# One fused Trainium2 kernel, its five queues in another order, its last token rows evicted in two parts and two early evictions moved to VectorE

## The chip, the cores and the metric

The kernel runs on one core of one Trainium2 chip. The core has five engines with a queue each, worked off strictly in order: TensorE (PE in the profile, its weight loads PEld), VectorE (DVE), ScalarE (ACT), GpSimd (POOL) and SyncE (SP), which here only issues DMA transfers. The metric is the device time of one execution in microseconds, as the median of several runs.

## What is computed

One transformer-like block on 2048 tokens of width 640, in bfloat16: a layer norm of `x`, a long convolution gated by it, a residual; then a layer norm and a gated feed-forward network of width 1728 with a residual.

```python
k_shift = sum over t of k_pad[:, t:t + S, :] * shift_k[:, ks - 1 - t]      # ks = 4 taps
kv = k_shift * v
y = irfft(rfft(kv, 2 S) * rfft(ssm_k, 2 S))[:S] + kv * ssm_D               # along the tokens
h = x + layernorm(x) * y
out = h + (silu(n @ w_gate) * (n @ w_up)) @ w_down      with n = layernorm(h)
```

## The kernel before

The 2048 tokens are four blocks of 512. Each block goes through the same stages:

- `kv(i)` (L673): k comes in transposed (`kT`), four taps are applied as matmuls with diagonal matrices in three groups (two 128-column pairs, then one alone); ScalarE evicts each group to `kT` (L700 in block 0, L717 later). In block 0 TensorE transposes them back and VectorE multiplies by v into `vt` (L713). In blocks 1 to 3 five DMA transposes (`kvt`, L486) bring them into `kvo`, and VectorE multiplies by v into `vt` (L726).
- `xfwd(i)` (L728): Fourier matmuls of `vt` with the table `ftab` into `XH[i]` (matmuls L584, evictions L597, butterflies L554; block 2 uses the shorter form, L622, L628, L632).
- `prod(j, i)` (L745): VectorE multiplies block j's spectrum with filter spectrum `C[i-j]` and adds into `Y` (L755, L756, L761, L771). The last product is followed by butterflies into `IO` and `IE`.
- `inverse(i)` (L819): inverse Fourier matmuls from `IE` and `IO` (L832), gating with the normalized x, the second layer norm's statistics on ScalarE (L870, L872), VectorE and GpSimd (L883), and four DMA transposes (`hn`, L486) into `hnT`.
- `ffn(i)` (L898): 13 groups of gate and up matmuls (L913, L914) and one half-size group (L924); per group ScalarE evicts silu(gate) (L936) and up (L938, into one of two buffers `ub` in turn), VectorE multiplies (L940). Then the down projection by token rows j = 0, 2, 1, 3 (L956), with one small paired matmul group for rows 0 and 2 and one for rows 1 and 3 (L968). Blocks 0 to 2 evict it by ScalarE (L976) and add on VectorE (L983); block 3 does both in one VectorE instruction (L986). One DMA per row writes the output (L990).

Ahead of that, `kload`, `ktrans` and `kfwd` (called kt0 to kt3 and kf0 to kf3 here) make the filter spectra `C[m]`, and `ln1(i)` makes the first layer norm.

PSUM is four tiles of two banks. A TensorE task that opens a tile waits until the tile's former users have read it.

Every `g.add(...)` makes a task, numbered as it is made. `ORDER` lists for each engine the numbers in the order in which its queue holds them. `schedule` walks through these lists with costs and latencies written down in the code; it assigns PSUM tiles, and it puts small filler matmuls (L249) into TensorE's waits that it foresees in the first stages. It doesn't change the order. `emit` turns data dependencies into semaphore waits. So a task waits for its data, and everything behind it in the same queue waits too.

The task numbers that matter below:

| tasks | what they are |
|---|---|
| 20, 24, 28 / 21, 25, 29 | block 0's three conv groups on TensorE / their evictions |
| 22, 26, 30 / 23, 27, 31 | their transposes on TensorE / products with v on VectorE |
| 137 to 148 | statistics of block 0's four token rows: two halves and an aggregation each, on VectorE |
| 110 to 113, 130 to 133 | last butterflies of kf2 and kf3 on VectorE |
| 128 / 129 | last Fourier group of kf3 / its eviction |
| 182, 188 / 183, 189 | butterflies into the two halves of `IO` / of `IE`, block 0 |
| 190 to 193 | inverse matmuls of block 0 (191 and 193 read `IO`) |
| 363 to 370 | product of blocks 0 and 1 |
| 338, 271, 279 | a small step of ln1 and two gate products of ff0 on VectorE |
| 297, 301, 306 | down projection of block 0, rows 2, 1 and 3 |
| 302 | paired group for rows 1 and 3 of block 0, opens a tile |
| 515, 516, 517 | block 2's third conv eviction, the DMA transpose of what it wrote, the product into `vt` that needs this transpose |
| 573 | a product of blocks 1 and 2 on VectorE (L755) |
| 536 to 550, even | Fourier matmuls of block 2 |
| 436, 442, 448, 454 | gate products (436, 448) and silu evictions (442, 454) of ff1 |
| 501, 710, 779 | last residual of block 1, load of block 3's x, a product on VectorE (L771) |
| 636, 637, 638, 730 | ff2's second gate-and-up group, its silu and its up eviction; a statistics pass of ln3 |
| 679, 683, 690 / 836 | the last gate products and the last small one of ff2 / a gating product of inverse 3 |
| 691, 692, 693 | down projection of block 2, row 0 in two pieces; pair of rows 0 and 2 |
| 804 to 807 | inverse matmuls of block 3, rows 0 to 3 |
| 814, 824, 828, 839 | ScalarE steps of block 3's second layer norm |
| 825, 816, 843, 834 | the four DMA transposes hn3, rows 1, 0, 3 and 2 |
| 892, 896 | block 3's 13th gate-and-up group and the half-size one |
| 906, 909, 913 / 907, 910, 914 | block 3's evictions of rows 0, 2, 1 / their output DMAs |
| 915, 916, 917 | row 3: matmuls, eviction, output DMA |

Of the kernel before, what the change touches and what calls it, by code (L numbers as in the profile page):

```python
# [10 lines left out]
ALU = mybir.AluOpType  # L11
ACTF = mybir.ActivationFunctionType
P = 128
# [10 lines left out]
class _Task:  # L24
    __slots__ = ("eng", "fn", "cost", "lat", "deps", "after", "succ", "npred", "ready", "end", "start",
                 "opens", "tiles", "idx", "clock", "sem", "seq", "dma", "name", "gap", "lock", "fill", "late", "pause")
# [32 lines left out]
class _Graph:  # L59
# [38 lines left out]
    def add(self, eng, name, fn, cost, r=(), w=(), pr=(), pw=(), skip=(), lat=None, dma=None, after=(), lock=None):  # L98
        t = _Task()
# [10 lines left out]
        t.late = set()  # L110
        t.seq = len(self.tasks)
# [118 lines left out]
    def emit(self, block):  # L230
# [85 lines left out]
    """,  # L316
    "act": """
# [12 lines left out]
    """,  # L330
    "dve": """
# [10 lines left out]
    """,  # L342
    "pool": """
        5 6 10 11 8 7 9 151 202 195 209 205 216 198 212 219 134 336 135 421 403 394 412 529 610 628 601 619 736 822 813 840
        831
    """,
    "sp": """
# [722 lines left out]
```

## Time and profile before

| | us |
|---|---|
| median of 3 runs | 270.15 |
| lowest and highest | 269.49, 270.49 |
| the profiled execution's own time | 269.68 |
| its span, first to last instruction | 267.8 |
| TensorE busy | 254.6 |
| ScalarE busy | 206.8 |
| VectorE busy | 201.7 |
| GpSimd busy | 28.7 |

The granted clock of TensorE was 0.998 over the span. The stages overlap: the filter spectra and block 0's transform fill the first 52 us, ff0 begins at 52.11, ff1 at 112.54, ff2 at 169.15 and ff3 at 219.91; the last matmul group starts at 260.87. In the profile a row of the timeline gives start and duration in microseconds, engine, line, operation, output and inputs by name, the shape, and in brackets the idle time before it with what ended that. In a row of grouped instructions the numbers behind the bar are busy time, mean nanoseconds of one, and idle time before them. In a row of waits the numbers are the sum, the count and the longest.

### The profile page before, as it was taken

To read this page: it belongs to the slowest core of one execution; us is meant where nothing else is said; L and a number is where in the kernel's file an instruction comes from. 1 tells how busy PE (TensorE), PEld (TensorE's weight loads), DVE (VectorE), ACT (ScalarE), POOL (GpSimd) and SP (SyncE) were. 2 spreads that over 40 slices of the span, in tenths; PEclk is the share of its full clock that TensorE was granted. 3 is DMA by queue.
4 is the path that set the end of the run, shared out by engine and by line. 5 is a ranking of instruction groups with operands and counts; after the bars stand their busy time and mean duration, and the time that the engine had idled before them with its cause. 6 is when DMAs were issued, how large, how long until landed. Compare 5 with 4: busy or idle time off the path is not lost.

```text
span 267.8 us, 4162 instructions
## 1 busy us (share of the span) xinstructions
PE 254.6 (95%) x1635; PEld 140.1 (52%) x1635; DVE 201.7 (75%) x282; ACT 206.8 (77%) x394; POOL 28.7 (11%) x37
## 2 busy tenths in 40 slices
PE   7899898999999998899899999999999989999995
PEld 5466563445445655444346567544446654444563
DVE  1599999999999998899999999999994000042204
ACT  2799999989887979948989997689799965346400
POOL 1000306011140042000040202000200200000000
PEclk9999999999999999999999999999999999999999
DMA  6999809959755637452000445500000150010004
GB/s 171 345 351 379 316 16 257 143 119 321 137 94 102 103 77 147 98 183 88 2 0 3 100 83 137 174 0 1 0 2 0 19 82 0 0 51 0 0 2 148
DMA packets 43557, 28.47 MB, mean 106 GB/s; under 512 B 32273, under 2 KB 41234, under 8 KB 43538
## 3 DMA queue, kind: packets, MB, share of 16 engines
q1 hardware_dynamic: 41824, 25.58, 35.4%
q0 software_dynamic: 1056, 2.62, 5.4%
q8 instruction: 13, 0.21, 0.3%
q10 hardware_dynamic: 658, 0.01, 0.1%
q14 instruction: 6, 0.05, 0.1%
HBM read 15.69 MB, written 2.62 MB: 68 GB/s over the span
## 4 chain that ended last, share of the span: by engine, by line
PE 41%; ACT 32%; DVE 15%; DMA 5%; SPq 2%; issue 2%; POOL 1%; ACTq 0%; DVEq 0%
PE ps L913 13%; PE ps L914 13%; PE ps L956 8%; PE ps L584 5%; ACT xh L815 4%; ACT ub L938 3%; ACT qo L856 3%; DMA vt<-in_A_v_dram 3%; DVE T L755 3%; ACT qo L872 3%; ACT qo L870 2%; DVE T L761 2%; ACT KT L545 2%; ACT gu L936 2%; DVE gu L940 2%; ACT qo L888 2%
## 5 line engine op out<-in xcount | busy, mean ns | idle before, releaser
L956 PE MATMUL ps<-Wd,gu 128*128 128x384 bf16 (+1 forms) x416 | 59.1, 300 | 0.1
L913 PE MATMUL ps<-hnT,GA 128*128 128x512 bf16 x140 | 53.1, 379 | 1.2 <-DMA hnT<-qo 0.7
L914 PE MATMUL ps<-hnT,UA 128*128 128x512 bf16 x140 | 53.1, 379 | 0.0
L956 PEld LDWEIGHTS ps<-Wd,gu 128*128 128x128 bf16 x416 | 39.9, 98 | 18.1 <-issue 1.6
L913 PE MATMUL ps<-hnT,GB 128*128 128x512 bf16 x120 | 45.5, 379 | 0.7 <-ACT gu L936 0.7
L914 PE MATMUL ps<-hnT,UB 128*128 128x512 bf16 x120 | 45.5, 379 | 0.0
L936 ACT ACTIVATE gu<-ps 128x512 bf16<-128x512 f32 x52 | 30.6, 598 | 17.8 <-PE ps L914 17.6
L938 ACT ACTIVATE ub<-ps 128x512 bf16<-128x512 f32 (+1 forms) x60 | 33.1, 566 | 6.6 <-PE ps L914 3.4
L940 DVE TENSOR_TENSOR gu<-gu,ub 128x512 bf16<-128x512 bf16 x52 | 21.0, 419 | 22.2 <-ACT ub L938 19.6
L755 DVE TENSOR_TENSOR T<-X,C 128x2560 bf16<-128x2560 bf16 x20 | 29.7, 1486 | 0.3
L756 DVE TENSOR_TENSOR T<-X,C 128x2560 bf16<-128x2560 bf16 x20 | 29.7, 1485 | 0.1
L913 PEld LDWEIGHTS ps<-hnT,GA 128*128 128x128 bf16 x140 | 13.7, 98 | 18.1 <-DMA hnT<-qo 1.0
L883 POOL TENSOR_TENSOR mv<-mv,half 128x1 f32<-128x1 f32 x16 | 15.3, 965 | 70.7 <-ACT mv L876 70.7
L584 PE MATMUL ps<-KT,ftab 128*128 128x320 bf16 x128 | 20.5, 301 | 2.0 <-DMA ftab<-cst_ftab 0.9
L914 PEld LDWEIGHTS ps<-hnT,UA 128*128 128x128 bf16 x140 | 13.7, 98 | 15.5
L913 PEld LDWEIGHTS ps<-hnT,GB 128*128 128x128 bf16 x120 | 11.7, 98 | 15.5 <-ACT gu L936 1.7
L761 DVE TENSOR_TENSOR T<-T 128x1280 bf16<-128x1280 bf16 x24 | 19.3, 819 | 0.2
L914 PEld LDWEIGHTS ps<-hnT,UB 128*128 128x128 bf16 x120 | 11.7, 98 | 13.8
L806 POOL TENSOR_TENSOR st<-st,half 128x8 f32<-128x8 f32 x4 | 9.1, 2267 | 91.2 <-ACT st L800 91.2
L771 DVE TENSOR_TENSOR Y<-Y,T 128x2560 bf16<-128x2560 bf16 x12 | 17.8, 1485 | 0.1
L584 PEld LDWEIGHTS ps<-KT,ftab 128*128 128x128 bf16 x128 | 10.3, 97 | 10.7 <-DMA ftab<-cst_ftab 1.4
L815 ACT ACTIVATE xh<-xh,st 128x640 bf16<-128x640 bf16 x16 | 14.5, 933 | 1.6 <-DVE st L808 1.6
(94 smaller groups left out, 372.8 us busy)
## 6 DMA issues: line engine op xcount, KB each, us to landing
kc<-in_A_ssm_k_dram SPq DMA_DIRECT2D x4, 640.0 KB, 9.2
xh<-in_A_q_dram SPq DMA_DIRECT2D x4, 640.0 KB, 4.2
vt<-in_A_v_dram SPq DMA_DIRECT2D x4, 640.0 KB, 6.3
out_dram<-xh SPq DMA_DIRECT2D x16, 160.0 KB, 1.9
Wd<-in_B_w_down_dram SPq DMA_DIRECT2D x1, 1280.0 KB, 6.5
C<-C POOLq DMA_DIRECT2D x1, 1280.0 KB, 13.6
C<-R POOLq DMA_DIRECT2D x1, 1280.0 KB, 9.4
UA<-in_B_w_up_dram SPq DMA_DIRECT2D x1, 1120.0 KB, 9.1
```

What stands on the lines that cost most here:

```text
L584: last = e.matmul(pt.f(c, W), ftab[:, cs, j, f * P:(f + 1) * P], src[:, j, c * W:(c + 1) * W], start=(j == par), stop=(j == par + 2))
L755: g.add("dve", nm, lambda e, x=x, k=k, t1=t1: e.tensor_tensor(out=t1, in0=x, in1=k, op=ALU.mult), cdve(2560), r=[x, k], w=[t1])
L756: g.add("dve", nm, lambda e, x=x, k=ksw, t2=t2: e.tensor_tensor(out=t2, in0=x, in1=k, op=ALU.mult), cdve(2560), r=[x, k], w=[t2])
L761: g.add("dve", nm, lambda e, p=p, q=q, d=d, op=op: e.tensor_tensor(out=d, in0=p, in1=q, op=op), cdve(1280), r=[p, q], w=[d])
L771: g.add("dve", nm, lambda e, y=y, z=z: e.tensor_tensor(out=y, in0=y, in1=z, op=ALU.add), cdve(2560), r=[y, z], w=[y])
L815: g.add("act", nm, lambda e, j=j, xj=xj: e.activation(out=xj, in_=xj, func=ACTF.Identity, scale=s[:, 4, j:j + 1], bias=s[:, 5, j:j + 1]), ...
L913: e.matmul(pt.f(0, N), wg[:, c, f0:f0 + P], hnT[:, c, :], start=(c == 0), stop=(c == NC5 - 1))
L914: last = e.matmul(pt.f(1, N), wu[:, c, f0:f0 + P], hnT[:, c, :], start=(c == 0), stop=(c == NC5 - 1))
L936: g.add("act", nm, lambda e, pt=pt, gv=gv, a=ps_g, ts=ts: e.activation(out=gv, in_=pt.f(a[0], N, a[1])[:, ts], func=ACTF.Silu, scale=gain) ...
L938: g.add("act", nm, lambda e, pt=pt, uv=uv, a=ps_u, ts=ts: e.activation(out=uv, in_=pt.f(a[0], N, a[1])[:, ts], func=ACTF.Copy, scale=gain) ...
L940: g.add("dve", nm, lambda e, uv=uv, gv=gv: e.tensor_tensor(out=gv, in0=gv, in1=uv, op=ALU.mult), cdve(n), r=[gv, uv], w=[gv])
L956: last = e.matmul(pt.flat(c1 - c0, P + c0), slots[fb][:, j * P:(j + 1) * P], Wd[:, fb, c0:c1], start=(fb == 0 and not second), stop=(fb == ...
```

## The change

All five queues get another order. Two evictions (tasks 21 and 129) go from ScalarE to VectorE, by a list `VECTOR` and a helper `evict` that stands in for the `g.add("act", ...)` calls of the filter, conv and transform evictions. The down projection of the very last token rows (block 3, j = 3) is split into columns 0 to 383 and 384 to 639, each with its own 13 matmuls, VectorE eviction and output DMA: tasks 915 to 917 and 918 to 920. The costs that the planner writes down for loads and transposed loads are other numbers, which set nothing on the chip but the choice of PSUM tiles, the filler matmuls and a few extra waits on VectorE. Three more places (a buffer `ZB`, the sign of `neg` and the subtraction at L847) depend on lists (`ACC`, `ST`) that hold no entry for them, so they add no instruction.

```diff
 ORDER = {
     "pe": """
-        13 35 32 24 20 28 49 43 41 22 39 47 26 51 37 65 30 45 164 162 160 158 63 60 170 168 166 108 172 84 78 58 76 68 72 82
...
+        13 32 35 20 24 28 22 41 43 37 47 51 26 39 49 45 30 65 160 162 164 158 172 168 170 166 58 63 60 80 68 84 76 86 78 70 82
...
-        345 343 349 244 357 353 355 256 351 268 252 260 264 276 284 272 280 386 388 291 387 385 292 506 510 293 514 301 302
-        297 306 550 542 540 546 536 548 429 544 538 425 437 445 433 441 453 461 469 449 457 477 465 473 593 595 484 592 594
...
+        347 349 244 256 355 351 357 264 353 252 260 268 276 272 280 284 386 388 387 385 291 506 292 510 293 514 297 301 302
+        536 306 540 550 538 542 548 425 546 544 429 445 437 433 453 449 441 461 457 469 477 465 473 593 595 594 484 592 485
...
-        680 684 805 807 804 691 692 806 693 701 697 702 706 844 848 864 868 852 860 856 872 876 880 884 888 896 892 903 904
-        905 911 908 912 915
+        684 805 807 804 691 806 692 693 701 702 706 697 868 856 848 864 844 852 860 876 884 872 888 880 892 896 903 904 905
+        911 912 908 915 918
     "act": """
...
-        814 824 815 829 841 830 842 832 833 698 707 694 845 846 849 850 703 865 853 854 862 861 857 858 866 877 873 874 870
...
+        739 681 678 673 740 674 685 686 817 689 688 835 682 819 808 820 810 821 837 811 823 812 838 826 824 814 828 839 815
...
     "dve": """
-        12 15 16 137 138 139 34 140 141 142 143 144 145 23 146 147 27 31 53 148 54 55 56 149 174 175 178 179 180 176 181 177
-        184 185 182 187 186 152 153 188 183 90 189 88 201 194 208 215 93 206 91 199 89 213 92 220 363 364 112 366 110 132 365
-        111 130 133 113 131 325 326 324 235 368 367 239 243 369 359 251 370 360 371 372 247 373 374 361 362 375 337 255 379
...
+        12 16 15 34 21 137 138 139 140 141 142 143 23 144 27 145 146 31 147 53 55 54 56 148 174 149 175 178 179 176 181 180
+        177 152 185 184 187 186 153 188 182 189 183 201 90 215 194 208 88 129 206 89 220 91 199 92 213 93 130 363 364 365 366
+        367 112 110 132 326 325 324 235 111 113 239 243 133 131 368 369 359 251 370 360 247 372 371 259 373 361 374 362 375
...
-        871 883 891 879 899 887 902 895 909 913 906 916
+        863 871 879 875 887 883 891 899 895 902 906 909 916 913 919
     "sp": """
...
-        504 508 505 512 509 513 424 516 397 296 406 415 309 300 305 503 712 711 716 715 720 613 719 723 489 498 631 604 622
-        502 493 710 825 816 843 834 700 696 910 709 705 907 914 917
+        231 505 509 508 513 512 516 406 397 424 415 305 300 309 296 503 711 712 720 715 716 719 723 613 622 604 631 489 498
+        493 502 710 825 816 843 834 907 709 700 705 696 917 910 914 920
...
+VECTOR = """
+    21 129
+"""
...
+        def evict(name, out, src, n, w, pr, scale=1.0, bias=None, r=(), after=()):
+            if len(g.tasks) in on_vector:
+                if bias is None and scale == 1.0:
+                    fn = lambda e: e.tensor_copy(out=out, in_=src())
+                elif bias is None:
+                    fn = lambda e: e.tensor_scalar(out=out, in0=src(), scalar1=scale, scalar2=None, op0=ALU.mult)
...
+                t = g.add("dve", name, fn, cps(n), r=r, w=w, pr=pr)
+            else:
+                kw = {"func": ACTF.Copy} if bias is None else {"func": ACTF.Identity, "bias": bias}
+                t = g.add("act", name, lambda e: e.activation(out=out, in_=src(), scale=scale, **kw), cact(n, bias is not None),
+                          r=r, w=w, pr=pr, after=after)
...
+                for c0, c1 in ((0, 3 * P), (3 * P, D)) if tail else ():
...
+                        for fb in range(last_fb):
+                            last = e.matmul(pt.flat(c1 - c0, P + c0), slots[fb][:, j * P:(j + 1) * P], Wd[:, fb, c0:c1],
+                                            start=False, stop=(fb == last_fb - 1))
...
+                    g.add("dve", nm, lambda e, pt=pt, xs=xs, m=m, c0=c0, c1=c1: e.scalar_tensor_tensor(
+                        out=xs, in0=pt.flat(c1 - c0, P + c0), scalar=m, in1=xs, op0=ALU.subtract, op1=ALU.add),
+                          cps(c1 - c0) + 60, r=[xs, m], w=[xs], pr=[pt])
+                    g.add("sp", "out%d" % i, lambda e, xs=xs, od=od[:, c0:c1]: e.dma_start(od, xs), 350, r=[xs], dma=((c1 - c0) * 0.74, 0), lat=1000)
```

More of the change, by code (lines that the diff above doesn't have):

```diff
@@ L25 @@
     __slots__ = ("eng", "fn", "cost", "lat", "deps", "after", "succ", "npred", "ready", "end", "start",
-                 "opens", "tiles", "idx", "clock", "sem", "seq", "dma", "name", "gap", "lock", "fill", "late", "pause")
+                 "opens", "tiles", "idx", "clock", "sem", "seq", "dma", "name", "gap", "lock", "fill", "late", "pause", "alt")
 class _Tile:
@@ L110, in add @@
         t.late = set()
+        t.alt = None
         t.seq = len(self.tasks)
@@ L544, in ktrans @@
                 dst = KT[m][:, jj:jj + 3:2, :]
-                g.add("act", "kt%d" % m, lambda e, pt=pt, dst=dst: e.activation(out=dst, in_=pt.h2(D), func=ACTF.Copy), cact(1280),
-                      w=[dst], pr=[pt], after=first_act)
+                evict("kt%d" % m, dst, pt_view(pt, lambda p: p.h2(D)), 1280, [dst], [pt], after=first_act)
                 if m == 0 and jj == 0:
@@ L675, in kv @@
             if i == 0:
-                tload("kT0", kT[:, :, 16:N + 16], K2[0:N, :], N, D, 2400)
+                tload("kT0", kT[:, :, 16:N + 16], K2[0:N, :], N, D, 1700, wait=700)
             else:
@@ L699, in kv @@
                 if i in PT:
-                    g.add("act", nm, lambda e, pt=pt, ks=ks, nb=nb: e.activation(out=ks, in_=pt.f2(N)[:, 0:nb], func=ACTF.Copy),
-                          cact(N * nb), w=[ks], pr=[pt])
+                    evict(nm, ks, pt_view(pt, lambda p, nb=nb: p.f2(N)[:, 0:nb]), N * nb, [ks], [pt])
                     tp = g.tile("kt")
@@ L753, in prod @@
                 t1, t2 = pair(u[0], u[1]), pair(u[2], u[3])
-                out = [T[:, u[0]], T[:, u[2]]] if j else [y[:, i % 2], y[:, 1 - i % 2]]
+                far = (j, i) in ACC and i == 3
+                out = [T[:, u[0]], T[:, u[2]]] if j and not far else [(ZB[:, f2] if far else y)[:, c] for c in (i % 2, 1 - i % 2)]
                 g.add("dve", nm, lambda e, x=x, k=k, t1=t1: e.tensor_tensor(out=t1, in0=x, in1=k, op=ALU.mult), cdve(2560), r=[x, k], w=[t1])
@@ L812, in ln1 @@
                       r=[s[:, 0, :]], w=[s[:, 2, :]])
+            if i in ST and i > 1:
+                neg = s[:, 4:6, :]
+                g.add("dve", nm, lambda e: e.tensor_scalar(out=neg, in0=neg, scalar1=-1.0, scalar2=None, op0=ALU.mult), 76, r=[neg], w=[neg])
             for j in range(4):
@@ L843, in inverse @@
                 st, bn = i in ST, (i, j) in BN2
-                assert not (st and i > 1)
                 if st:
```

53 lines of the change are left out of this document (35 added, 18 removed), and 41 rows, old and new, of the table ORDER.

## The prediction

> **What bounds the kernel now.** I read the page first (busy shares, the slices, the instruction-fetch queue, the chain of work that ended last), then the busy time by stretches.
>
> ```profile
> span 267.8 us, 4162 instructions
> PE 254.6 (95%) x1635; PEld 140.1 (52%) x1635; DVE 201.7 (75%) x282; ACT 206.8 (77%) x394; POOL 28.7 (11%) x37
> DVE  1599999999999998899999999999994000042204
> ACT  2799999989887979948989997689799965346400
> q8 instruction: 13, 0.21, 0.3%
> PE 41%; ACT 32%; DVE 15%; DMA 5%; SPq 2%; issue 2%; POOL 1%; ACTq 0%; DVEq 0%
> ...
> core 0: us, PE busy (x) PEld busy (x) DVE busy (x) ACT busy (x) POOL busy (x), PEclk, DMA share, GB/s
> 12.80:54.00 41.20, 38.33 (x318) 22.71 (x317) 39.84 (x58) 40.96 (x67) 6.80 (x9) 1.00 0.85 243
> 46.00:85.00 39.00, 38.92 (x216) 18.82 (x213) 38.69 (x52) 34.83 (x68) 5.68 (x4) 1.00 0.80 164
> 105.00:140.00 35.00, 33.45 (x170) 15.82 (x168) 33.54 (x43) 28.85 (x58) 3.51 (x2) 1.00 0.28 77
> 220.00:253.00 33.00, 32.91 (x163) 15.55 (x165) 7.52 (x19) 16.83 (x33) 0.00 (x0) 1.00 0.03 10
> ```
>
> TensorE's row is full nearly everywhere, but three engines share the bound. From 12.8 to 54 us ScalarE is busy 40.96 of 41.20 us and VectorE 39.84: TensorE waits there for PSUM tiles to be evicted. From 46 to 85 TensorE (38.92 of 39.00) and VectorE (38.69) are both full, and until 140 VectorE stays so. Only from about 200 on is VectorE free. So a new order is worth what it takes out of TensorE's queue, and only where VectorE or ScalarE do not end last anyway. The waits of TensorE after 52 us, by what ended them:
>
> ```profile
> PE ps L968 <- ACT kT L717: 1.1, 1, 1.1
> PE ps L913 <- ACT gu L936: 0.7, 2, 0.6
> PE ps L913 <- DMA hnT<-qo: 0.7, 1, 0.7
> PE ps L913 <- ACT FO L628: 0.5, 1, 0.5
> PE ps L693 <- ACT qo L856: 0.2, 1, 0.2
> PE ps L622 <- ACT FO L628: 0.2, 1, 0.2
> PE ps L968 <- DVE gz L940: 0.2, 1, 0.2
> ```
>
> They sum to 1.1 + 0.7 + 0.7 + 0.5 + 3 x 0.2 = 3.6 us. That is all a perfect order could win between 52 us and the last matmul; the first 52 us and the tail come on top.
>
> **The change part by part.** I sum against the profiled execution's own 269.68 us (span 267.8 and 1.9 around it); the median of the runs is 270.15, 0.47 above it.
>
> *The first 52 us.* Two evictions leave ScalarE: task 21 (first conv pair, 1024 columns) and task 129 (last eviction of kf3, 640 columns).
>
> ```profile
> 13.43 1.03 DVE L786 BATCH_NORM_STATS2 bst<-xh 128x6 f32<-128x320 bf16 x2
> 14.96 1.23 DVE L713 TENSOR_TENSOR vt<-ps,vt 128x1024 bf16<-128x1024 f32 x1 [0.26 <-PE ps L584]
> 35.77 0.82 DVE L554 TENSOR_TENSOR IE<-Y 128x1280 bf16<-128x1280 bf16 x1
> 35.91 2.35 PE L832 MATMUL ps<-IO,itab 128*128 128x320 bf16 x16
> L597 ACT ACTIVATE KO<-ps 128x640 bf16<-128x640 f32 x16 | 12.1, 790 | 1.7 <-PE ps L584 1.7
> 52.11 0.38 PE L913 MATMUL ps<-hnT,GA 128*128 128x512 bf16 x1
> ```
>
> Task 21 falls before 12 us, when ScalarE would wait for the tables anyway; its gain is that task 29 slips in front of that wait, some 0.6 us. Task 129 saves 0.6 to 0.8 (a 640-column eviction lasts 0.79, overlapped with its neighbours). So ScalarE's full stretch shrinks by about 1.3 us. Against that, VectorE used to fill its wait for v (which ends at 14.96, task 23) with both halves of the third token row's statistics and their aggregation (143 to 145); now only the first half stands before 23, and 0.5 + 0.2 us move behind it. And the half of IO that was done early (task 182) now follows task 188, so the first inverse matmul, which started at 35.91 and needs both halves, starts 0.75 later (one 0.82 step, overlapped). VectorE also carries task 129, bounded by 0.5 (statistics of 320 columns) and 1.23 (1024 columns); I take 0.8. The hidden-state loads come back to about the old 52 us because their four steps are spread better; then 0.8 more on a full VectorE meets the first Fourier tasks of block 1, and between block 1's conv product and its inverse VectorE now has four butterflies of kf2 and kf3 more (111, 113, 133, 131; 0.75 each with the overlap, 3.0) and one product (367, 1.4) and three small steps (0.9) less: the inverse of block 1 is due 0.7 later. ScalarE's gain of 1.3 shows in it only in part, by some 0.3. Sum until that inverse: **+0.4**, ends -1.0 (all of ScalarE's 1.3 arrives, less small losses) and +1.2 (none does).
>
> *Down-projection of block 0, block 2's conv and transform (88 to 115 us).*
>
> ```profile
> 101.87 0.45 PE L968 MATMUL ps<-Wd,gz 64*128 64x384 bf16 x4 [1.09 <-ACT kT L717]
> 102.24 7.24 PE L956 MATMUL ps<-Wd,gu 128*128 128x384 bf16 x52
> 109.49 1.32 PE L622 MATMUL ps<-vt,ftab 128*128 128x320 bf16 x8
> 112.54 0.38 PE L913 MATMUL ps<-hnT,GA 128*128 128x512 bf16 x1 [0.49 <-ACT FO L628]
> 103.33 1.93 SPq L486 DMA_TRANSPOSE hnT<-qo  x1
> 105.30 1.27 SPq L486 DMA_TRANSPOSE kvo<-kT  x1
> 108.47 0.96 DVE L726 TENSOR_TENSOR vt<-vt,kvo 128x1536 bf16<-128x1536 bf16 x1 [1.12 <-DMA kvo<-kT]
> ```
>
> The 1.09 at 101.87 (task 302 wants a tile) goes: 297, a group of 3.6 us that needs no new tile, now stands ahead of 301 and 302. But task 536 of the transform moves in front of the group 306. It reads all of vt, whose last product ends at 108.47 + 0.96 = 109.43 in the old run. SyncE now issues the last conv transpose (516, old start 105.30) ahead of the hidden-state transposes, no longer behind the one that waited until 103.33 and took 1.93; its data were evicted at 101.8, so it comes some 3.5 us sooner, to land near 108.5 - 3.5 + 0.4 = 105.4. With its product vt is done at 106.4 if VectorE is free; 573, which stands before it, can add up to 1.5. TensorE reaches 536 at the old start of 306, 102.24 + 3.6 = 105.8, less the 1.1, plus the 0.4: 105.1. A new wait of 1.3 to 2.8; I take 1.3. ScalarE's evictions still pace the rest (0.49 and 0.2 stay). So -1.1 + 1.3, less 0.3 for hn1's last piece, which is ready earlier: **-0.1**, ends -1.9 (all three waits gone) and +3.8 (the transfer is no earlier; the rival below).
>
> *Blocks 1 to 3 up to 200 us.* The 0.7 of L913 behind L936 comes from gate halves that stand far back on ScalarE, whose partner buffer waits for VectorE. Task 436 moves ahead of 448, 442 ahead of 454: **-0.3**, ends -0.7 and +0.4. Block 3's eight transform tasks now all precede 636, and 638, the up half of 636, stands after 730; a tile is held longer, while x3's load (710) is queued behind 501, which moves behind 779 (1.49 on VectorE): **+0.2**, ends -0.2 and +1.0, by what one 0.8 to 0.9 us statistics pass in front of an eviction can cost.
>
> *The last inverse and hn3.*
>
> ```profile
> 212.47 6.03 SPq L486 DMA_TRANSPOSE hnT<-qo  x4
> 215.53 3.71 PE L956 MATMUL ps<-Wd,gu 128*128 128x384 bf16 x26
> 219.91 0.39 PE L913 MATMUL ps<-hnT,GA 128*128 128x512 bf16 x1 [0.68 <-DMA hnT<-qo]
> 252.02 0.66 PEld L956 LDWEIGHTS ps<-Wd,gu 128*128 128x128 bf16 x6 [0.42 <-DVE gu L940]
> ```
>
> SyncE's four transposes run back to back, 6.03 us from 212.47, so the last is as late as the first (825 waits for 824). 824 moves ahead of 839, 828 and 814 on ScalarE, 1.3 us of work, and 806 moves ahead of 692. The last transpose then waits for its own data and lands about 1 us sooner: **-0.7**, ends 0 and -0.7, as TensorE has other work until 219.2. The 0.2 at the gz pair goes, since 690 is no longer behind 836, 679 and 683: **-0.2**. At 252.02 weights waited 0.42 for the last gate group; 892 now precedes 896, a full 1.1 us of cover: **-0.2** (the matmuls lost less than the weights). Both at worst 0.
>
> *The tail.*
>
> ```profile
> 260.60 2.60 DVE L986 SCALAR_TENSOR_TENSOR xh<-ps,st,xh 128x640 bf16<-128x640 f32 x3 [8.63 <-PE ps L956]
> 261.51 4.35 SPq L990 DMA_DIRECT2D out_dram<-xh  x6
> 264.62 0.88 DVE L986 SCALAR_TENSOR_TENSOR xh<-ps,st,xh 128x640 bf16<-128x640 f32 x1 [1.42 <-PE ps L956]
> DMA to landing us min/median/max: 1.8/1.9/2.2
> ```
>
> The last eviction shrinks from 640 columns to 256. By 1.23 for 1024 and 0.88 for 640, a column costs 0.9 ns, so 0.53 remains: -0.35. The same 26 matmuls and weight loads run, in another order. On VectorE 913 (0.88) runs between 916 and 919 while TensorE finishes: no delay. On SyncE the last four issues follow 917, which waits for 916 at about 263.7; old issues took 4.35/6 = 0.7 with waits inside, so the last is due between 265.0 and 265.7, against data at 265.15. The last transfer carries 64 KB instead of 160; all old ones were 160 KB (1.8 to 2.2), so between 0 and 0.4 is saved, I take 0.2. **-0.55**, ends 0 and -0.75. [...]
>
> Sum: 0.4 - 0.1 - 0.3 + 0.2 - 0.7 - 0.2 - 0.2 - 0.55 = -1.45, so 268.2 on the profiled execution's basis and 270.15 - 1.45 = **268.7** on that of the runs.
>
> **The rivals.**
>
> *The joints close better than I count.* The whole 3.6 of waits, half of ScalarE's 1.3 and the tail go: 3.6 + 0.65 + 0.55 = 4.8; with one new wait like the 1.3 left in, -3.5: 266.65. For it: most of the rows above are single waits with a neighbour to swap in. Against: VectorE is full until 184.
>
> *Nothing but the end moves.* VectorE sets the middle (38.69 of 39.00; 33.54 of 35.00), gets 0.8 more and keeps its work; what TensorE wins before 140 it waits for later. Left are hn3, gz, 252 and the tail, 1.65, less the 0.4 of the start and the 0.8 of the extra eviction: -0.45, 269.7. It includes that the change does not do what it says: orders built around fetches win nothing, because fetches cost nothing. The fetch queue took 0.3% of the DMA time and "issue" is 2% of the chain. The Trainium skill ("Runtime: NRT & Kernel Launch", section "Instruction fetch mechanics") says that fetches are sequential and mostly hidden; by that rule this rival would be right for that part of the change, and the trace agrees.
>
> *Slower: 536 holds TensorE.* In-order TensorE meets 536 before 306. If vt is finished no earlier than the old 109.43, TensorE stands from 104.7 (105.8 - 1.1) for 4.7 us, with the 3.6 us group 306 queued behind, and ff1 and all later blocks behind that. The other terms bring 1.45 + 1.3 = 2.75, so the kernel is slower from 2.75 us of waiting on. At full price: 4.7 - 2.75 = +1.95, 272.1. For it: the transfer, the conv eviction and one ordering on VectorE (517 after 573) must all come early. Against: SyncE's order does bring it early.
>
> **How the numbers follow.** Forecast 0.38, joints better 0.24, only the end 0.20, slower 0.18. A median of this kernel can be told from no change at about 0.5%, 1.35 us: faster is below 268.8, slower above 271.5. The forecast's own range is 267.2 to 270; a little over half of it is faster: 0.38 x 0.55 + 0.24 + 0.20 x 0.05 = 0.46. Slower: 0.18 x 0.9 + small shares of the others = 0.19. Same: 0.35. The range, 266.0 to 271.8, leaves out a tenth on each side.
>
> **What would show it.** TensorE's first L832 matmul near 36.7 and first L913 near 52; the wait of L968 behind kT L717 gone, and a wait of L622 behind vt L726 of about 1.3 in its place; no wait of L913 for hnT near 219; the last L986 about 0.5 us long with 256 columns. I am wrong if the L622 wait is over 2.75 us, if VectorE gets idle time before 140, or if new waits over 0.6 appear between 165 and 200.

## The result, and the profile after

| | before | after |
|---|---|---|
| median of 15 runs | 269.97 us (269.21 to 270.49) | 268.70 us (266.93 to 269.99) |
| after / before | | 0.9954, 95% interval 0.9938 to 0.9971 |
| profiled execution | 269.68 us, span 267.8 | 268.22 us, span 266.3 |

The change makes the kernel 0.46% faster: the interval excludes 1, but the gain is just inside the half per cent that the prediction called no change. The median is the predicted one, from a median of before that is 0.18 us below the 270.15 of three runs from which the prediction started, so the medians differ by 1.27. The two profiled executions differ by 1.46 us where the sum said 1.45. The parts of that sum are another matter, as the stages show. Of all runs used below, one of the kernel with 292 first and the exchange was slow, at a granted clock of 0.993, and is left out of its median, and four of the twelve with the evictions back on ScalarE had a clock of 0.994 and 271.1 to 271.7 us, without which their median would be 269.59. The page of after, in the lines that answer to those of before:

```profile
span 266.3 us, 4177 instructions
PE 254.0 (95%) x1638; PEld 142.1 (53%) x1638; DVE 204.0 (77%) x285; ACT 203.9 (77%) x392; POOL 29.1 (11%) x37
DVE  0889999999999999999999999999895101330404
ACT  2689999999967999766979999678799982653600
q8 instruction: 13, 0.21, 0.3%
PE 53%; ACT 23%; DVE 11%; DMA 6%; SPq 4%; issue 2%; POOL 0%; DVEq 0%
```

ScalarE has lost 2.9 us of work and VectorE has gained 2.3; TensorE's share of the chain that ended last rose from 41% to 53%. Busy time by stretches of after (the columns are those of the table in the prediction):

```profile
12.80:54.00 41.20, 36.67 (x312) 23.66 (x310) 39.20 (x57) 39.69 (x65) 6.95 (x9) 1.00 0.81 231
46.00:85.00 39.00, 39.00 (x227) 19.40 (x220) 38.14 (x48) 34.22 (x65) 6.11 (x4) 1.00 0.84 179
105.00:140.00 35.00, 34.58 (x179) 16.71 (x178) 34.62 (x47) 26.57 (x55) 1.89 (x1) 1.00 0.21 53
```

From 12.8 to 54 us ScalarE is busy 1.27 us less than before, close to the 1.3 of the prediction, and VectorE 0.64 less. Between 105 and 140 TensorE is busy 34.58 us instead of 33.45. What TensorE waits for from 54 us on (us in total, times, longest):

```profile
PE ps L941 <- DMA hnT<-qo: 1.1, 1, 1.1
PE ps L717 <- DMA kT<-in_A_k_dram: 0.6, 1, 0.6
PE ps L860 <- ACT qo L884: 0.4, 1, 0.4
PE ps L941 <- ACT FO L502: 0.2, 1, 0.2
```

Four waits, 2.3 us, instead of eight with 3.6. The large ones of before (a tile for task 302, the gate evictions of block 1, the hidden state of block 3) are gone. Two new ones stand in their place, both behind a transfer. Where they are, in TensorE's timeline of after (start, us):

```profile
36.64 1.65 PE L860 MATMUL ps<-IO,itab 128*128 128x320 bf16 x11
...
52.54 0.38 PE L941 MATMUL ps<-hnT,GA 128*128 128x512 bf16 x1
...
94.37 1.06 PE L717 MATMUL ps<-kT,dg 64*64 64x512 bf16 x16 [0.61 <-DMA kT<-in_A_k_dram]
...
106.06 0.45 PE L647 MATMUL ps<-vt,ftab 128*128 128x320 bf16 x2
...
112.17 0.39 PE L941 MATMUL ps<-hnT,GA 128*128 128x512 bf16 x1 [0.20 <-ACT FO L502]
...
170.05 0.39 PE L941 MATMUL ps<-hnT,GA 128*128 128x512 bf16 x1 [1.09 <-DMA hnT<-qo]
...
219.17 0.38 PE L941 MATMUL ps<-hnT,GA 128*128 128x512 bf16 x1
```

The start of TensorE's first matmul in each stage, in both traces, cuts the 1.46 us into the prediction's terms (ff1 is block 1's up-projection, xf3 block 3's Fourier stage):

| stretch | before | after | change | predicted |
|---|---|---|---|---|
| start to block 1's inverse | 85.77 | 86.11 | +0.34 | +0.4 |
| to ff1 (112.54, 112.17) | 26.77 | 26.06 | -0.71 | -0.1 |
| ff1 to block 2's inverse (143.27, 141.86) | 30.73 | 29.69 | -1.04 | -0.3 |
| to xf3 (165.87, 164.45) | 22.60 | 22.59 | -0.01 | 0 |
| xf3 to block 3's inverse (199.39, 199.21) | 33.52 | 34.76 | +1.24 | +0.2 |
| to ff3 (219.91, 219.17) | 20.52 | 19.96 | -0.56 | -0.9 |
| to TensorE's end (264.58, 263.57) | 44.67 | 44.40 | -0.27 | -0.2 |
| TensorE's end to the end of the span | 3.20 | 2.75 | -0.45 | -0.55 |

Five terms hold within 0.35. Two gains are larger than predicted, by 0.6 and 0.7, and one loss by 1.0: these errors nearly cancel. The experiments ask first for that loss.

### The profile page after: what moved, and what is told of

Its sections match the earlier page's. It is cut to its first block, busy times and chain, and to the rows that moved or that the text cites. A ratio compares the mean times of both kernels' runs of the same rounds, so it can differ in the third digit from the quotient of the medians.

```text
span 266.3 us, 4177 instructions
## 1 busy us (share of the span) xinstructions
PE 254.0 (95%) x1638; PEld 142.1 (53%) x1638; DVE 204.0 (77%) x285; ACT 203.9 (77%) x392; POOL 29.1 (11%) x37
## 4 chain that ended last, share of the span: by engine, by line
PE 53%; ACT 23%; DVE 11%; DMA 6%; SPq 4%; issue 2%; POOL 0%; DVEq 0%
PE ps L941 16%; PE ps L942 15%; PE ps L1003 14%; SPq L514 3%; ACT xh L843 3%; ACT KT L502 3%; PE ps L610 2%; DMA kT<-in_A_k_dram 2%; ACT KO L502 2%; DMA ftab<-cst_ftab 2%; DMA hnT<-qo 2%; DVE gu L968 2%; PE ps L717 2%; ACT C L502 1%; ACT qo L884 1%
## 5 line engine op out<-in xcount | busy, mean ns | idle before, releaser
L1003 PE MATMUL ps<-Wd,gu 128*128 128x384 bf16 (+1 forms) x390 | 55.5, 299 | 0.1
L1003 PEld LDWEIGHTS ps<-Wd,gu 128*128 128x128 bf16 x390 | 37.6, 98 | 17.1 <-issue 1.1
L966 ACT ACTIVATE ub<-ps 128x512 bf16<-128x512 f32 (+1 forms) x60 | 33.9, 567 | 14.9 <-PE ps L942 12.0
L911 POOL TENSOR_TENSOR mv<-mv,half 128x1 f32<-128x1 f32 x16 | 16.1, 1010 | 69.1 <-ACT mv L904 69.1
L610 PE MATMUL ps<-KT,ftab 128*128 128x320 bf16 x128 | 19.8, 300 | 3.5 <-ACT KT L502 1.1
L831 POOL TENSOR_TENSOR st<-st,half 128x8 f32<-128x8 f32 x4 | 8.3, 2067 | 88.1 <-ACT st L825 88.1
L610 PEld LDWEIGHTS ps<-KT,ftab 128*128 128x128 bf16 x128 | 11.2, 98 | 10.9 <-ACT KT L502 2.0
```

The lines of the kernel that those rows point to most:

```text
L610: last = e.matmul(pt.f(c, W), ftab[:, cs, j, f * P:(f + 1) * P], src[:, j, c * W:(c + 1) * W], start=(j == par), stop=(j == par + 2))
L966: g.add("act", nm, lambda e, pt=pt, uv=uv, a=ps_u, ts=ts: e.activation(out=uv, in_=pt.f(a[0], N, a[1])[:, ts], func=ACTF.Copy, scale=gain) ...
L1003: last = e.matmul(pt.flat(c1 - c0, P + c0), slots[fb][:, j * P:(j + 1) * P], Wd[:, fb, c0:c1], start=(fb == 0 and not second), stop=(fb == ...
```

## The experiments

Each kernel was timed beside the kernel before on the same chip. The ratios below are to that one; the changed kernel's own is 0.9954 (0.9938 to 0.9971). The median of before was 269.70 to 269.97 us from one time to the next, so a difference of 0.3 us between medians taken at different times says nothing.

In several of these traces the record of the first matmul of an up-projection is missing. Its start is then taken from the weight loads: where both are recorded, the second load begins within 0.01 us of the first matmul (170.06 and 170.05 us in after).

### What holds block 2's up-projection

In the trace of after the last hidden-state transpose of block 2 (task 631) is issued at 165.69 and lands at 170.00; fifteen of its sixteen parts are in by 168.38. The DMA queues between 167.85 and 168.95 us (packets, MB, share of 16 engines), and the four transposes of that stage, which land 2.6 us after their issue except for one:

```profile
q1 hardware_dynamic: 232, 0.27, 73.5%
q8 instruction: 1, 0.02, 5.7%
```

```profile
DMA to landing us min/median/max: 2.6/2.6/4.3
```

At 167.91 us one packet of 16 KB of instructions was fetched; 5.7% of sixteen engines over 1.1 us is one engine for 1.0 us. The 13 packets of q8 are TensorE's: 252 of its instructions on average lie between two of them. So the suspicion is that the sixteenth part stood behind this fetch; the profile does not show which engine moved the part. Three kernels test it. The first two move the fetch and leave the transposes where they are.

```diff
-                for k in range(WARM):
-                    last = e.matmul(pt.f(k % 2, N // 2), z[:, 0:P], z, start=True, stop=True)
+                for k in range(48):
+                    last = e.matmul(pt.f(k % 2, 128), z[:, 0:P], z[:, 0:128], start=True, stop=True)
```

> The changed kernel with 48 warm-up matmuls of 128 columns instead of 24 of 256: the same warm-up work, but 48 more instructions (matmuls and weight loads) on TensorE ahead of everything, so that TensorE's instruction fetches come 48 instructions earlier in its program; the fetch that stood at 167.91 us moves to about 164.5. Theory (the wait of 1.1 us for hnT at 168.66 is the last transpose of block 2, one of whose sixteen parts stood behind that fetch: 170.00 instead of 168.4): the wait falls under 0.4 us and the kernel gets 0.8 to 1.3 us faster than the changed one, about 267.6. Rival (the transpose is late because the order gives it its data late, or because the stores of block 1 stand right behind it): the wait stays at 1.1, and the time at 268.7.

```diff
+                for k in range(12):
+                    last = e.matmul(pt.f(k % 2, N), z[:, 0:P], z.unsqueeze(1).to_broadcast([P, 2, N // 2]), start=True, stop=True)
```

> The changed kernel with 12 warm-up matmuls of 512 columns instead of 24 of 256: 24 instructions fewer, so that the fetch at 167.91 us moves to about 169.5, behind the data of block 2's last transpose (all other parts in at 168.38). Theory of the fetch: the wait for hnT near 168.7 is under 0.3 us, and the kernel 0.8 to 1.3 us faster, about 267.6, unless the other fetches, which move too, hit other transposes. Rival (late data, or the stores behind): wait 1.1 us and time as in the changed kernel.

The third leaves the fetch and moves the transpose, by one exchange on SyncE:

```diff
-  613 622 604 631
+  613 622 631 604
```

> The changed kernel with one exchange in SyncE's order: the last two hidden-state transposes of block 2 swapped (631, whose data is ready at 162.93, ahead of 604, whose data is ready at 164.43). TensorE's program and its fetches stay where they are. Theory (the wait for hnT before block 2's up-projection is made by the fetch at 167.9 falling into the data phase of the last transpose): the last one now lands at about 167.4, ahead of the fetch; the wait of 1.1 us is gone, and the kernel 0.8 to 1.1 us faster than the changed one, about 267.8. Rival (the wait belongs to the transposes' own length or to late data): the last transpose lands at 169.0 or later and over 0.5 us of wait stays.

| kernel | fetch | last hnT lands | ff2 after xf3's start | median | ratio to before |
|---|---|---|---|---|---|
| after | 167.91 | 170.00 | 5.60 us | 268.70 | 0.9954 (0.9938 to 0.9971) |
| earlier fetch | 164.61 | 169.75 | 4.35 us | 268.71 | 0.9958 (0.9942 to 0.9973) |
| later fetch | 170.05 | 167.99 | 4.41 us | 268.21 (profile: 266.69) | 0.9948 (0.9927 to 0.9968) |
| exchange on SyncE | 167.85 | 167.94 | 4.37 us | 267.41 | 0.9911 (0.9892 to 0.9930) |

The wait is gone in all three, and the stretch is 1.2 us shorter in each (the 1.09 of the wait is counted from the modelled end of the matmul before). The other kernels bear it out: in the five profiles in which a fetch meets this last transpose, after among them, the stretch takes 5.46 to 5.60 us, and in the seven others with the changed order 4.35 to 4.48. The four transposes with the exchange, and TensorE at that place (its first up-projection matmul has no record here and starts with the second weight load, at 169.27):

```profile
DMA to landing us min/median/max: 2.6/2.6/2.6
```

```profile
165.70 3.69 PE L612 MATMUL ps<-vt,ftab 128*128 128x320 bf16 x26
169.26 0.10 PEld L943 LDWEIGHTS ps<-hnT,GA 128*128 128x128 bf16 x1 [0.19 <-ACT FO L504]
169.49 0.38 PE L944 MATMUL ps<-hnT,UA 128*128 128x512 bf16 x1
```

The last matmul of xf3 runs straight into the up-projection. The rivals fall: the other transposes are no shorter, the stores of block 1 still stand right behind the last, and the data is no earlier than before, only the order of two transfers (the last is issued 0.40 us after xf3's start instead of 1.24, since SyncE no longer waits for the data of 604 ahead of it). The exchange also gives a kernel faster than both: its interval lies below that of the changed kernel.

The two kernels with shifted fetches won that time and lost much of it elsewhere, because every fetch moves. With the earlier one, the fetch that stood at 105.30 came at 100.77, in the middle of block 2's conv transposes. Their landing times (window 94 to 106 us), and VectorE and TensorE after it:

```profile
DMA to landing us min/median/max: 2.4/2.5/3.9
```

```profile
103.19 0.42 DVE L748 TENSOR_TENSOR vt<-vt,kvo 128x512 bf16<-128x512 bf16 x1 [1.41 <-DMA kvo<-kT]
...
106.12 0.96 DVE L748 TENSOR_TENSOR vt<-vt,kvo 128x1536 bf16<-128x1536 bf16 x1
```

```profile
107.14 0.45 PE L647 MATMUL ps<-vt,ftab 128*128 128x320 bf16 x2 [1.41 <-DVE vt L748]
```

That is the wait of task 536 for `vt` that the prediction had priced at 1.3; here it is 1.41. With the later fetch, TensorE waited 1.4 us for block 2's k instead of 0.6.

### Task 536 ahead of 306

```diff
-  513 512 516 406 397 424 415
+  513 512 406 397 516 424 415
```

> The changed kernel with the last conv transpose of block 2 (516, into kvo) moved in SyncE's order from ahead of the hidden-state transposes 406 and 397 to behind them, close to where it stood before. Theory of the prediction's slower rival (536 stands ahead of the group 306 on TensorE and reads all of vt; in the changed kernel vt is done at 105.48 and 536 starts at 106.06, with no wait): 516 lands at about 109.2, vt is done near 110.2, TensorE waits some 4 us for vt from 106.1 on, and the kernel is 2.7 to 4.0 us slower than the changed one, 271.4 to 272.7. Rival (536's place is harmless, other work absorbs it): within 0.5 us of 268.7.

Measured 272.06, ratio 1.0088 (1.0058 to 1.0117): 3.4 us slower than the changed kernel, as expected. TensorE at that place:

```profile
106.43 0.45 PE L1017 MATMUL ps<-Wd,gz 64*128 64x384 bf16 x4
106.81 3.31 PE L250 MATMUL ps<-ident 128*128 128x192 bf16 x38
110.33 0.45 PE L649 MATMUL ps<-vt,ftab 128*128 128x320 bf16 x2 [0.21 <-DVE vt L750]
```

The planner saw this wait coming and put 38 filler matmuls into it (L250, they compute nothing that is used; it does so beyond the first stages too), so a list of waits shows only 0.21 of the 3.52 us. So 536's place costs no wait as long as the transpose lands in time. Two other stretches of this profile differ and nearly cancel: TensorE waits 0.9 us longer for block 2's k, and from block 2's inverse to ff2 it takes 0.7 less; no fetch meets the last transpose there, since with the fillers in the program the one at 167.91 comes at 165.59.

The other new wait, for k at 94.37, was attacked by covering it:

```diff
-  385 291 506 292 510 293 514
+  385 291 292 506 510 293 514
```

> The changed kernel with one move on TensorE: the 6 matmuls of task 292 (1.0 us, down-projection of block 0, no new tile) ahead of conv task 506, as they stood before the change. Theory (at 93.48 TensorE waits 0.78 us for k's transpose of block 2, and 1.3 to 1.7 in the runs in which an instruction fetch falls later into that transpose): the wait goes or falls by up to 1.0 us, and the time by 0.5 to 1.0 us, to about 267.9. Rival (conv evictions on ScalarE and the transposes of kvo then set the next wait, 536 behind vt): vt comes 0.2 to 1.0 us later, a wait of L647 behind vt takes the place, and the time stays at 268.7.

> The same move of task 292, together with 12 warm-up matmuls of 512 columns instead of 24 of 256 (the kernel with the later fetches, 268.2, whose only large wait left was 1.4 us for k's transpose of block 2). Theory: both waits, for hnT near 168 and for kT near 93, are gone or under 0.5 us, and the time is 266.8 to 267.4. Rival (a wait for vt takes the place of the one for kT): 268.0 or more.

> The same exchange on SyncE and the move of task 292 ahead of conv task 506 on TensorE, in the changed kernel. Theory: the gains add, since they lie in different blocks (0.9 for the exchange, 0.6 to 1.4 for the move): 266.4 to 267.0, faster than either kernel and than the move alone (267.27). Rival (what TensorE wins in block 0 it waits for later): 267.3 or more.

| kernel | median | ratio to before | block 1's inverse to ff1 |
|---|---|---|---|
| 292 first | 267.27 (7 runs) | 0.9918 (0.9885 to 0.9951) | 26.44 us |
| 292 first, later fetch | 267.46 (7 runs) | 0.9912 (0.9881 to 0.9944) | 26.53 us (26.83 with the later fetch alone) |
| 292 first, exchange on SyncE | 267.24 (5 runs) | 0.9920 (0.9888 to 0.9952) | 28.29 us |

The last column has to be read with k's transpose beside it: with 292 first it took 6.6 and 6.7 us from issue to landing, with a fetch that met it late, and 6.5 with the later fetch alone, but only 5.7 in the profile of the changed kernel, whose stretch takes 26.06. At equal length of that transpose, then, the move is worth 0.5 us: 26.44 against 26.97 in the profile of the kernel with the old joint of block 3 (6.6 us too; it follows below), and with the later fetch 0.3, with a transpose that is 0.2 longer. The rest of the 1.0 hoped for is taken back by a wait of 0.5 us for `vt` before 536, in both profiles. The median of the move alone lies 1.4 us under that of the changed kernel, but the intervals overlap, and its profile has the gain elsewhere, in a first stage that is 1.5 us shorter (first inverse matmul at 35.15). With the exchange on top the median is 267.24, between the 267.0 of the theory and the rival's 267.3, and not shown to be faster than either edit alone. In its profiled execution, of 269.23 us, the gain is lost here:

```profile
105.36 0.45 PE L1017 MATMUL ps<-Wd,gz 64*128 64x384 bf16 x4
108.11 0.45 PE L649 MATMUL ps<-vt,ftab 128*128 128x320 bf16 x2 [2.31 <-DVE vt L750]
```

Here the fetch at 104.94 fell into transpose 516, which took 4.6 us instead of 2.4. How often that meeting happens from run to run, and so whether the gains add without it, stays open.

### The evictions, the joint of block 3 and the tail by themselves

```diff
 VECTOR = """
-    21 129
 """
 VectorE
-  15 34 21 137
+  15 34 137
...
-  88 129 206
+  88 206
 ScalarE
-  33 36 25 29
+  33 36 21 25 29
...
-  211 127 318 109
+  211 127 129 318 109
```

> The changed kernel with the two early evictions (tasks 21 and 129) back on ScalarE, everything else in the changed order. Theory of the prediction (ScalarE's full stretch shrinks by 1.3 us, of which some 0.3 arrives, and VectorE pays 0.8 for task 129): within 0.4 us of the changed kernel, 268.3 to 269.1. Rival (ScalarE alone sets the first 52 us): 1.0 to 1.3 us slower, about 269.9, with the first up-projection matmul at 53.5 instead of 52.54.

Measured 269.88, ratio 1.0016 (0.9992 to 1.0040): 0.9 to 1.2 us slower than the changed kernel. The profiled executions differ by 1.7 (spans 268.0 and 266.3) and split it: the first up-projection matmul comes at 53.21, 0.67 later, and then TensorE waits longer for k. The first part is not chance: from the first inverse matmul to it this profile takes 16.52 us, and the eleven others with the changed order 15.86 to 15.90.

```profile
96.07 1.06 PE L718 MATMUL ps<-kT,dg 64*64 64x512 bf16 x16 [1.58 <-DMA kT<-in_A_k_dram]
```

So the evictions themselves are worth 0.7, between the theory's 0.3 and the rival's 1.3; the other 1.0 is the transpose of k, which took 6.7 us from issue to landing, with a fetch at 91.73, instead of 5.7.

```diff
 ScalarE
-  826 824 814 828 839 815
+  826 814 828 839 824 815
 TensorE
-  691 806 692 693
+  691 692 806 693
```

> The changed kernel with the joint of block 3 as before: 824 behind 814, 828 and 839 on ScalarE, 806 behind 692 on TensorE. Theory (the prediction's 0.7 for the hidden-state wait at 219.9, measured 0.56 for the whole joint): a wait for hnT before block 3's up-projection of 0.5 to 0.9 us returns, and the kernel is 0.5 to 0.8 us slower than the changed one, about 269.3. Rival (that wait of before was the fetch at 213.15 in the first transpose, and the order does nothing): hnT as in the changed kernel, under 0.2 us of difference.

Measured 269.89, ratio 1.0004 (0.9989 to 1.0020), 1.2 us slower. The profiled executions differ by 1.8: 0.9 of it is block 2's k, which took 6.6 us with a fetch at 91.12, and from block 3's inverse to ff3 the stretch takes 20.91 us instead of 19.96. So the joint is worth 0.95, more than the theory said. But the wait for hnT did not come back; TensorE lost the time earlier:

```profile
204.78 1.90 PE L1005 MATMUL ps<-Wd,gu 128*128 128x256 bf16 x13
207.46 0.99 PE L1005 MATMUL ps<-Wd,gu 128*128 128x384 bf16 x6 [0.77 <-DVE gu L970]
```

With 692 ahead of 806, 692 waits for the last gate products of block 2. In the changed kernel the inverse 806 fills that time. The last transpose lands at 220.86 here, 0.08 us before TensorE comes for it at 220.94 (218.92 and 219.17 in after), so without that wait TensorE would have stood here for most of the same time. So the two edits probably win it only together; no run has one alone.

```diff
-                tail = i == NB - 1 and j == 3
+                tail = False
```

`ORDER` loses 918 to 920 with it, and 916 and 917 come last in their lists.

> The changed kernel with the last token row evicted whole again (640 columns, one store of 160 KB). Theory (tail split is worth 0.45 us, the difference of the two profiles between TensorE's last matmul and the span's end, 3.20 before and 2.75 after): 0.3 to 0.6 us slower than the changed kernel, about 269.1. Rival (the split only exchanges a shorter eviction for one more store in SyncE's queue): within 0.1 us of it, 268.7.

In the profile TensorE's end and the span's end are 3.21 us apart (263.74 and 266.95) where the split has 2.75: the 0.46 is there (2.74 to 2.76 in the eleven profiles with the split). In the medians it can't be told: 268.79 of 12 runs, ratio 0.9973 (0.9952 to 0.9993). Last evictions on VectorE, with the split and without:

```profile
262.19 0.62 DVE L992 SCALAR_TENSOR_TENSOR xh<-ps,st,xh 128x384 bf16<-128x384 f32 x1 [1.23 <-PE ps L985]
262.84 0.88 DVE L1033 SCALAR_TENSOR_TENSOR xh<-ps,st,xh 128x640 bf16<-128x640 f32 x1
263.64 0.47 DVE L992 SCALAR_TENSOR_TENSOR xh<-ps,st,xh 128x256 bf16<-128x256 f32 x1
```

```profile
263.78 0.89 DVE L1035 SCALAR_TENSOR_TENSOR xh<-ps,st,xh 128x640 bf16<-128x640 f32 x1 [1.86 <-PE ps L1005]
```

### Block 1's up-projection

```diff
 TensorE
-  425 546 544 429 445 437 433 453 449 441 461 457 469
+  429 546 544 425 437 445 433 441 453 461 469 449 457
 ScalarE
-  426 427 547 545 431 430 520 439 446 521 438 435 522 434 523 524 447 525 443 526 442
+  431 426 547 545 427 430 520 439 438 521 447 435 522 434 523 524 454 525 446 526 462
...
 VectorE
-  436 559 583 448 585 586 444 588 587 456 589 530 452
+  448 559 583 436 585 586 456 588 587 444 589 530 464
...
```

> The changed kernel with the tasks of block 1's up-projection (425 to 483) in the order of before among themselves, on TensorE, ScalarE and VectorE; all else in the changed order. Theory (the two waits of 0.72 and 0.32 us of TensorE for a gate half, at 127.97 and 130.85 before, went by this order alone): they come back, and block 1 takes 0.8 to 1.1 us more between its first up-projection matmul and block 2's inverse (112.17 to 141.86 in the changed kernel), the whole 0.5 to 1.1 us slower, about 269.6. Rival (they went because VectorE reached the products earlier, for reasons further up): under 0.3 us of difference.

The edit changes 10 places of TensorE's list, 22 of ScalarE's and 12 of VectorE's. Measured 276.59, ratio 1.0248 (1.0218 to 1.0278): 7.9 us slower, far from both expectations. The waits of TensorE between 112 and 160 us:

```profile
PE ps L943 <- ACT gu L966: 2.4, 2, 1.3
PE ps L1005 <- DVE gu L970: 1.4, 1, 1.4
PE ps L943 <- ACT X L504: 1.3, 1, 1.3
PE ps L862 <- ACT gz L966: 0.8, 1, 0.8
PE ps L943 <- ACT ub L968: 0.7, 1, 0.7
```

The likely reason is that the old order among these tasks does not fit the new places of the transform's evictions and products between them; then this kernel prices a mismatch, not the edit. The cleaner try was one small edit in the kernel before:

```diff
 VectorE
-  577 555 554 556 557 428 578 579 432 559 558 580 440 581
+  577 555 554 428 556 557 578 432 579 559 558 440 580 581
```

> The kernel before, with three gate products of block 1's up-projection placed earlier among the transform's products on VectorE: 428 behind 554, 432 behind 578, 440 behind 558 (2, 1 and 1 places of full steps earlier); nothing else. Theory (TensorE's waits of 0.72 us at 127.97 and 0.32 at 130.85 come from up buffers that VectorE frees late: 440 ends at 127.24, ScalarE's 447, 435 and 434 follow it, and 461 waits for 434): both waits are gone, 0.8 to 1.1 us of the time of before (269.9) go. Rival (VectorE is full, and the transform's products that come later hold block 2's inverse): waits gone, but the inverse starts no earlier than before's 143.27, time as before.

Measured 270.16, ratio 1.0019 (0.9998 to 1.0041), no gain. TensorE's waits between 112 and 144 us:

```profile
PE ps L916 <- ACT FO L630: 0.7, 1, 0.7
PE ps L915 <- ACT ub L940: 0.6, 1, 0.6
PE ps L915 <- ACT gu L938: 0.2, 1, 0.2
```

The first row stands ahead of ff1. The waits behind the gate became waits behind the up half, and the stretch from ff1 to block 2's inverse takes 30.85 us, 0.1 more than before. The theory of the three products falls. Which part of the new order took the 1.04 us away stays open; the stretch takes 29.69 in every profile that keeps it.

## Why the prediction was right

Its number is right partly by luck: three errors, of 0.6, 0.7 and 1.0 us, cancel but for 0.3, and the smaller ones take back that. By its steps:

- *The first 52 us, +0.4.* Measured +0.34, and the first inverse matmul came at 36.64 (36.7 predicted). The parts were right in sign: VectorE's wait for v is no longer filled, as this row of after shows,

```profile
15.28 1.23 DVE L736 TENSOR_TENSOR vt<-ps,vt 128x1024 bf16<-128x1024 f32 x1 [1.18 <-PE ps L610]
```

  where before had 0.26. But of the two evictions 0.3 was to arrive, and 0.7 did, so the rest of the new order costs that much more than was said. One part was left out: the 0.8 for task 129 on VectorE, which took 0.83 there (L494), is named but not in the sum, for its 0.7 is 3.0 - 1.4 - 0.9.
- *88 to 115 us, -0.1.* Measured -0.71. The wait of task 302 went, as said. The failed step is the 1.3 of 536: `vt` was finished at 105.48, since transpose 516 landed at 104.12 and not at 105.4, and TensorE came at 106.06, not at 105.1, mostly because it had waited 0.61 for k before 94.37. The prediction had no term for that wait. It named the right mechanism: moved back, it cost 3.4 us, and the rival's 272.1 was measured as 272.06. The size of this gain is in part luck of the profiled execution, in which k's transpose took 5.7 us: in four other profiles with the same order of this stretch (evictions on ScalarE, old joint of block 3, whole tail, exchange on SyncE) it took 6.2 to 6.7, and the stretch 26.59 to 27.02 us, that is 0.2 less to 0.25 more than before.
- *Blocks 1 to 3, -0.3 and +0.2.* The first is a term of the right sign and a third of the size: both waits went whole. The prediction took 0.7 as its bound, from the list of waits, which counts from the modelled end of the matmul before; from start to start, where 0.22 us is usual in these rows of before, the two cost 0.72 and 0.32:

```profile
127.97 0.38 PE L914 MATMUL ps<-hnT,UB 128*128 128x512 bf16 x1
128.90 0.39 PE L913 MATMUL ps<-hnT,GB 128*128 128x512 bf16 x1 [0.55 <-ACT gu L936]
...
130.85 0.38 PE L914 MATMUL ps<-hnT,UB 128*128 128x512 bf16 x1
131.39 0.39 PE L913 MATMUL ps<-hnT,GB 128*128 128x512 bf16 x1 [0.16 <-ACT gu L936]
```

  So the 3.6 us of waits were not all that an order could win. The second term failed outright: +1.24, with the wait of 1.1 before ff2. The prediction bounded it by a statistics pass in front of an eviction; in fact the last transpose met an instruction fetch. What it did count was of the right size: with the exchange this stretch takes 33.70 us, 0.18 more than before. The prediction had set a new wait over 0.6 between 165 and 200 us as what would make it wrong, and that came; another of its signs, idle time of VectorE before 140, came too (0.64 us less busy from 12.8 to 54, 0.55 from 46 to 85).
- *hn3 and gz, -0.9.* Measured -0.56 against the kernel before, and 0.95 when these two edits alone are undone in the changed kernel. No wait for hnT is left at 219.17. The difference is about the 0.35 us that inverse task 804 now waits for an eviction (L860 behind L884).
- *The last gate group, -0.2:* -0.27. *The tail, -0.55:* -0.45; the last eviction took 0.47 us (0.53 estimated), and the store of 64 KB, issued at 264.17, landed at 265.84, 1.67 later: 0.2 less than 1.9, as taken.

The rival "only the end moves" rested on fetches that cost nothing, since they take 0.3% of the DMA time. That ground is gone: the share is right and the conclusion is not, because a fetch can delay a transfer that is in flight. The Trainium skill ("Runtime: NRT & Kernel Launch", section "Instruction fetch mechanics") gives 16 KiB blocks of 256 instructions and calls the cost of crossing one mostly hidden. The block size agrees with the trace's 252 instructions. The cost does not where a fetch meets a transfer that TensorE needs next: it is not a stall of TensorE's own issue (2% of the chain, as before), but a late transfer, and the three kernels above put it at 1.2 us.

The new order does not keep the transfers clear of the fetches: in the profile of after, fetches fall into transposes of block 0 (47.33), block 1 (105.30), block 2 (167.91) and block 3 (213.21), and into k's (89.67); before, at 47.73, 89.45, 103.94 and 213.15. Only the one at 167.91 and k's show in the list of waits.

## What to carry to other kernels

A transfer on which TensorE waits next should be in before, or issued well after, the instruction fetch that its own program triggers at that place; where two transfers of a group become ready out of order, issue the ready one first, which here was worth 1.2 us by one exchange. A list of waits names the late transfer but not why it is late: compare its time from issue to landing with that of its neighbours, and look into the DMA queues at that moment. Gains at joints that lie in other blocks need not add, since every instruction put in or taken out of TensorE's program upstream, and every shift in time, moves the later fetches against the transfers.

## What was not expected of the hardware

- In the profile of after, 21 of the 24 hidden-state and conv transposes that no 16 KB fetch met took 2.3 to 2.7 us from issue to landing (the other three, up to 5.5, stood among weight loads at 44 to 57 us). The four that a fetch met first took 4.2 to 4.4, and those next in the queue 3.0 to 3.4; a fetch itself lasts 0.9 to 1.4. In three of the four, fifteen parts were on time and one was late: 168.38 and 170.00, 105.70 and 107.38, 213.72 and 215.58; the one of block 0 came late as a whole (49.41 to 49.48). The late part came 1.6 to 1.9 us behind the others, more than the 1.0 to 1.25 of these fetches; why stays open.
- Over all fourteen profiles a fetch met 27 transposes of blocks 1 to 3 at 1.8 to 2.6 us after their issue: 17 had one part late by 1.5 to 2.3 us, four came late as a whole (4.3 to 4.4 us), and six took their usual time.
- A load does it otherwise: in before, three conv transposes issued right behind a load of v (98.00 to 100.54 us) took 3.0 to 4.4 us without a fetch, and all sixteen parts of each came late together (102.38 to 102.44 for the first).
- It goes by the moment: with the exchange, the fetch began at 167.85, and the transpose that landed at 167.94 took its usual 2.6.
- The longer transpose of k in blocks 2 and 3 took 4.8 to 5.3 us without a fetch, 5.1 with a fetch 0.9 us after its issue, 5.4 to 5.9 with one after 1.1 to 1.3, and 6.2 to 6.7 with one after 2.2 to 4.1. In blocks 0 and 1, in the first 46 us, it took 5.6 to 6.8 without one. With a fetch 4.1 us after its issue, in block 3 of two kernels, one part came 1.5 us late (150.15 and 151.65 with the earlier fetch); block 2's came together (94.12 to 94.33 in after), so there the link with the fetch rests on these times alone.
- The changed kernel's runs spread over 3.1 us, those of before over 1.3. In the profile of the kernel with 292 first, v of block 0 landed at 13.38 with a fetch at 12.95, and the first inverse matmul came at 35.15; in that of the changed kernel it landed at 15.26 with a fetch at 13.20. Such meetings would explain the spread; no run here shows that they do.
